# A transformer block with local dilated attention and a SiLU MLP: other tiles for the modulation weights, another order of loads and instructions

## The chip, the cores and the metric

The kernel runs on one core of a Trainium2 chip. The core has a matrix engine (TensorE, PE), a vector engine (VectorE, DVE), a scalar engine (ScalarE, ACT), a general one (GpSimd, POOL) and a sync engine (SyncE, SP) that here only issues DMAs. Each engine runs its own list of instructions in order and waits on semaphores. Data lie in SBUF (128 partitions); matmul results land in PSUM, which this kernel uses as eight banks of 128 x 512 floats. The metric is device time in microseconds of one execution.

## What is computed

The reference, cut to its core (S = 2048 tokens, D = 448, 16 heads of 28, F = 1792, all bfloat16):

```python
mod = (silu(c) @ w_mod).reshape(1, 6, 1, 448)      # w_mod: 448 x 2688
sa, ca, ga, sb, cb, gb = the six rows of mod
h = layernorm(x) * (1 + ca) + sa
# attention: each query sees 8 keys, at distances 0, 2, 4 ... 14 back
o = softmax(q . k[s - 2w] * 28**-0.5 over w = 0..7) . v
x = x + ga * (o @ wo)
h = layernorm(x) * (1 + cb) + sb
x = x + gb * (silu(h @ w1) @ w2)
```

Because the dilation is 2, even and odd tokens never meet: the kernel handles the two parities as two sequences of 1024.

## The kernel before

**Tiling.** The tokens are cut into four chunks of 512 (256 per parity). Attention runs in nine blocks of queries per parity; a block's keys are the 128 tokens up to its last query, so that a dense 128-key product and a 0/1 mask (`maskb`) replace the gather. A dimension of 448 is three tiles of 128 rows and a rest of 64. For the matmuls with D as the contracted side (QK, V, output projection, first MLP matmul) a helper `phases` runs pairs of 64-row matmuls, so that the rests of the two parities or the two halves of the output share a tile: this is why the rest of the QK weights is `wqk3`, two 64-row halves in one 128-row tile, and that of w1 is `w13`. The modulation weights `wmod`, in contrast, lie as four tiles of 112 rows (`KM = 112`).

**Stages.** First `c` goes through SiLU (`sc_op`), is turned into columns by a matmul (`c_cols`) and copied to `scT`; `mod_first` multiplies it with the first two of the six column groups of `wmod` (32 matmuls with one column each, L444), giving the shift and scale of the first layernorm (`modc`, L447/L448). Meanwhile the first chunk of tokens is normalised (statistics L497/L498 on VectorE or sums L501 and squares L507 on ScalarE, the power on GpSimd L513, the result `xn` L525/L527), transposed by PE (L564) and scaled into `h` (L571/L573). The later chunks are transposed by DMA (L588) and scaled by L593/L595. The QK weights are copied from `wqk` and `wqk3` into `wp` and `wp3`, in which each head of 28 columns is padded to 32 (`pad`, L603/L605; four copies, each on ScalarE or VectorE). QK is L668, its copies out of PSUM L672; V is L688 and L681. For each block and parity: logits L716, exponentials L724 on ScalarE, mask L748 and, after the product with V (L774), the division L779/L780 on VectorE, and a DMA transpose into `oT` (L784). The output projection L804 needs the `oT` of both parities and `wo`, which is multiplied by the gate `ga` (L916, with copies L917/L918); its result is added to x (L807). The MLP is L831, SiLU L839, L854 and the last addition L859 with the store L862; `w2` is multiplied by the gate `gb` (L920) two tiles at a time. The other four column groups of `wmod` are multiplied in `mod_late` (L463 into one row each, copied L477, spread to all partitions L468/L480 as gates, or turned to columns L475).

**Order.** Nothing schedules at run time. The kernel makes a list of 764 operations, and the string `ORDER` says in which order they are emitted, on which engine the ones with a choice run (suffix v for VectorE, a for ScalarE) and which PSUM banks they take (after slashes). The DMA issues of SyncE are in this order too; SyncE has eight completion semaphores for them, so the ninth DMA waits for an earlier one to land. The numbers in `load` and other operations (assumed durations) are read only by a planner that makes such a string; for a given `ORDER` they do nothing. On PE, a few matmuls on zeros (`junk`, L416) fill the wait at the beginning.

Before the change SyncE issues, in this order: first tokens of chunk 0, `wmod`'s first part in two loads (two of the four 112-row tiles each), the tokens of chunk 1, `wqk3`, V's weights in two loads, the QK weights in two, the tokens of chunks 2 and 3, the transposes of chunk 1, the second part of `wmod`, the transposes of chunk 2, `wo`, w2's first part, w1's first, and so on. ScalarE issues the other tokens of chunk 0 and then `c`.

The two loads with 64-row halves read DRAM with the two halves as the leading dimension:

```python
load(112, wqk3[:], dram(A_wqkv, 128, D, ((128, -D, 2), (1, 0, K3), (0, 1, D))), late)
load(224, w13[:], dram(B_w1, 128, F // 2, ((128, -F // 2, 2), (1, 0, K3), (0, 1, F // 2))), late, rate=0.3)
```

A second copy of the whole layer (`safe`) runs only where a softmax sum was out of range; it is not taken here.

Of the kernel before, what the change touches and what calls it, by code (L numbers as in the profile page):

```python
# [10 lines left out]
ALU = mybir.AluOpType  # L11
# [11 lines left out]
KM = D // KT  # L23
# [56 lines left out]
def half(j):  # L80
    return slice(K3 * j, K3 * j + K3)
# [156 lines left out]
def layer(ctx, tc, io, safe):  # L238
# [26 lines left out]

    NV, NP, NX, NO, NH = (4, 5, 2, 3, 3) if not safe else (4, 3, 2, 2, 3)
    x_all = ct([128, 4 * NC, D], "x_all")
    c4 = ct([KT, KM], "c4")
    sc4 = ct([KT, KM], "sc4")

    both = ct([128, 2 * NF * 512], "both")
# [752 lines left out]
```

## Time and profile before

| | us |
|---|---|
| median of three runs | 171.03 (170.42 to 171.82) |
| the profiled execution | 170.89 |
| its span, first to last instruction | 169.2 |
| PE busy | 160.8 |
| ScalarE busy | 116.4 |
| VectorE busy | 99.1 |

The profile is one execution. Its lines name the engine, the line of the code, what is written from what, the shape and the count; a time after an arrow is idle time of that engine and what ended it. A "chain of waits" is followed back from the last instruction, at each step to what released it. A matmul's duration in a row is modelled from start to end, and neighbours overlap, so the rate of a group is read from a row of the chain or from the distance of its start to that of the next group. The tables of stages give for each engine its busy microseconds and its number of instructions, then the granted clock of PE, the share in which the 16 DMA engines were busy, and GB/s.

### The profile page before, as it was taken

What the parts mean: (1) busy time and instruction counts of PE and PEld (TensorE: products, weight loads), DVE (VectorE), ACT (ScalarE), POOL (GpSimd) and SP (SyncE); (2) the same over time, 40 slices, a digit from 0 to 9 for tenths busy, and PEclk for the clock granted to TensorE, in tenths of its full rate; (3) what the DMA queues carried; (4) which work ended last, traced back from release to release, by engine and by line L of the source; (5) the groups of instructions that cost most, each with busy time, mean ns of one, the idle gap of its engine ahead of it and who ended that gap; (6) DMA issues with size and microseconds to landing.
All of it is one profiled execution on the core that took longest, in us unless ns stands there. A gap on an engine that the chain in (4) does not pass through costs nothing.

```text
span 169.2 us, 4278 instructions
## 1 busy us (share of the span) xinstructions
PE 160.8 (95%) x1763; PEld 79.9 (47%) x1764; DVE 99.1 (59%) x259; ACT 116.4 (69%) x166; POOL 15.5 (9%) x38
## 2 busy tenths in 40 slices
PE   7878999999999999999999999999999999999990
PEld 2344444353465554554464454564444454444670
DVE  2788899999988859475476309972950405100120
ACT  3676999899779967879996989484429903248000
POOL 4313112010000410011000000021001100000000
PEclk9999999999999999999999999999999999999999
DMA  5994999859994453500614001226410061100022
GB/s 180 251 324 171 190 303 164 265 154 101 142 248 109 112 103 76 169 0 9 119 27 111 2 0 31 54 63 117 113 54 6 0 124 38 49 0 0 27 62 68
DMA packets 32312, 17.48 MB, mean 103 GB/s; under 512 B 24157, under 2 KB 31453, under 8 KB 32285
## 3 DMA queue, kind: packets, MB, share of 16 engines
q1 hardware_dynamic: 32132, 16.90, 42.9%
q8 instruction: 16, 0.26, 0.7%
q10 hardware_dynamic: 152, 0.23, 0.4%
q14 instruction: 12, 0.09, 0.2%
HBM read 9.12 MB, written 1.84 MB: 65 GB/s over the span
## 4 chain that ended last, share of the span: by engine, by line
PE 74%; DMA 9%; DVE 7%; ACT 5%; issue 2%; SPq 0%
PE psum L831 25%; PE psum L854 24%; PE psum L804 7%; PE psum L668 6%; DMA wqk<-in_A_wqkv_dram 5%; PE psum L688 4%; PE psum L774 4%; PE psum L716 2%; DMA x_all<-in_A_x_dram 2%; DMA oT<-o 2%; DVE p L748 2%; PE psum L885 2%; ACT both L501 1%; ACT wp L603 1%; DVE wqk L595 1%
## 5 line engine op out<-in xcount | busy, mean ns | idle before, releaser
L831 PE MATMUL psum<-h,w 64*128 64x512 bf16 x392 | 43.7, 376 | 0.0
L854 PE MATMUL psum<-w,both 128*128 128x448 bf16 x210 | 42.1, 353 | 0.0
L839 ACT ACTIVATE both<-psum 128x1024 bf16<-128x1024 f32 x28 | 27.3, 1021 | 13.6 <-PE psum L831 13.6
L724 ACT ACTIVATE p<-psum 128x896 bf16<-128x896 f32 (+1 forms) x36 | 31.7, 935 | 5.0 <-PE psum L716 4.7
L831 PEld LDWEIGHTS <-w 64*128 64x128 bf16 x392 | 19.3, 94 | 22.2 <-issue 0.7
L854 PEld LDWEIGHTS <-both 128*128 128x128 bf16 x210 | 19.6, 98 | 19.1 <-issue 1.6
L513 POOL TENSOR_TENSOR rs<-rs,negh 128x2 f32<-128x2 f32 x16 | 12.5, 778 | 118.0 <-DVE rs L510 82.6
L748 DVE TENSOR_TENSOR p<-p,maskb 128x1792 bf16<-128x1792 bf16 (+1 forms) x18 | 19.5, 1099 | 4.8 <-ACT p L724 4.8
L859 DVE TENSOR_TENSOR ot<-psum,x_all 128x448 bf16<-128x448 f32 x15 | 9.2, 618 | 20.2 <-PE psum L854 15.9
L668 PE MATMUL psum<-h,wp 64*128 64x512 bf16 x168 | 19.8, 377 | 0.5 <-ACT wp L603 0.4
L668 PEld LDWEIGHTS <-wp 64*128 64x128 bf16 x224 | 10.4, 94 | 12.8 <-ACT wp L603 0.9
L507 ACT ACTIVATE mrow<-x_all,mv 128x448 bf16<-128x448 bf16 x16 | 10.7, 668 | 3.4 <-DVE mv L504 3.0
L804 PE MATMUL psum<-wo,oT 64*128 64x448 bf16 x112 | 12.7, 350 | 0.1
L593 ACT ACTIVATE h<-h,modc 128x512 bf16<-128x512 bf16 x7 | 5.5, 806 | 10.2 <-DMA h<-xn 10.2
L672 ACT CAST qk<-psum 128x1024 bf16<-128x1024 f32 x12 | 12.0, 1018 | 0.6 <-PE psum L668 0.6
L688 PE MATMUL psum<-wv,h 64*128 64x448 bf16 x98 | 11.3, 350 | 1.2 <-DMA wv<-in_A_wqkv_dram 1.1
L807 DVE SCALAR_TENSOR_TENSOR x_all<-psum,x_all 128x448 bf16<-128x448 f32 x16 | 9.5, 619 | 3.6 <-PE psum L804 3.6
L780 DVE TENSOR_TENSOR o<-psum,rc 112x448 bf16<-112x448 f32 (+1 forms) x18 | 11.2, 624 | 0.6
L779 DVE RECIPROCAL rc<-psum 112x16 f32<-112x16 f32 (+1 forms) x18 | 4.5, 251 | 10.2 <-PE psum L774 9.5
L774 PEld LDWEIGHTS <-p 128*128 128x128 bf16 x288 | 8.2, 96 | 3.3 <-issue 1.7
L774 PE MATMUL psum<-v,p 128*128 128x29 bf16 x288 | 9.0, 176 | 0.0
L595 DVE TENSOR_SCALAR h<-h,modc 128x512 bf16<-128x512 bf16 x17 | 6.1, 406 | 4.8 <-DMA h<-xn 4.6
(95 smaller groups left out, 144.6 us busy)
## 6 DMA issues: line engine op xcount, KB each, us to landing
out_dram<-ot SPq DMA_DIRECT2D x16, 112.0 KB, 1.8
both<-in_w_mod_dram SPq DMA_DIRECT2D x1, 1568.0 KB, 8.4
x_all<-in_A_x_dram SPq DMA_DIRECT2D x3, 448.0 KB, 8.1
w<-in_B_w_dram SPq DMA_DIRECT2D x3, 448.0 KB
w<-in_B_w_dram SPq DMA_DIRECT2D x1, 896.0 KB, 7.0
both<-in_w_mod_dram SPq DMA_DIRECT2D x2, 392.0 KB, 5.7
w<-in_B_w_dram SPq DMA_DIRECT2D x1, 672.0 KB, 5.4
wv<-in_A_wqkv_dram SPq DMA_DIRECT2D x2, 224.0 KB, 8.5
```

The source lines that it names most:

```text
L513: G.tensor_tensor(out=rs[:, j:j + n], in0=rs[:, j:j + n], in1=negh[:, 0:n], op=ALU.pow)
L668: return T.matmul(ps[:, j, :], lhsT=w.rearrange("p h d -> p (h d)"), rhs=h[rows, :, t, 128:128 + CP], start=start, stop=stop)
L672: copy_on(o)(out=qk[:, :, g, :, s0:s0 + CP], in_=ps.rearrange("p j (t s) -> p j t s", t=2))
L688: T.matmul(ps[:, par, 0:D], lhsT=h[rows, par, t, b0:b0 + 128], rhs=wv[rows, t, :], start=start, stop=stop)
L724: S.activation(out=out_, in_=ps[:, :, 0:4 * nq].rearrange("p j (g q) -> p j g q", q=nq), func=ACTF.Exp, scale=SCALE)
L748: V.tensor_tensor(out=p, in0=p, in1=maskb[:, 1 if b == 0 else 0, 0:nq].unsqueeze(1).to_broadcast([128, H, nq]), op=ALU.mult)
L774: T.matmul(ps[:, h, 0:DH + 1], lhsT=p[:, at:at + 128], rhs=v[:, h, 0:DH + 1], start=True, stop=True)
L780: V.tensor_tensor(out=box["o"][0:nq, off:off + D].rearrange("p (h d) -> p h d", d=DH), in0=ps[0:nq, :, 0:DH], in1=r.unsqueeze(2).to_broadc ...
L804: T.matmul(ps[par][:, 0:D], lhsT=oT[rows, t, par, s0:s0 + 128], rhs=wo[rows, par, t, :], start=start, stop=stop)
L831: return T.matmul(ps[:, j, :], lhsT=w, rhs=h[rows, :, t, :], start=start, stop=stop)
L839: silus[k].append(P.op(("act", 904.0), lambda o, i=i, box=box: S.activation(out=hid[:, k % 2, :, i, :], in_=box["ps"], func=ACTF.Silu), [m ...
L854: T.matmul(box["ps"][:, 0:D], lhsT=hid[:, k % 2, f % 2, f // 2, 128 * j:128 * j + 128], rhs=w2[:, f // 2 + 7 * (f % 2), :], start=(f == 0) ...
```

## The change

`wmod`'s 448 rows become three tiles of 128 and one of 64 (`KM = 64` is now the width of a piece of `c`, of which there are seven, turned into columns by two matmuls). The fourth tile's other 64 rows are set to zero by two new memsets of VectorE, and the modulation matmuls contract over 128 rows. The first and the second part of `wmod` are each two loads, one of three tiles and one of 64 rows. `wqk3` and `w13` are loaded by two DMAs each, one for each half. The tokens of chunk 1 are issued after V's weights, those of chunks 2 and 3 in one load; two 448 KB loads of w1 become one, and the two of w2 become one. ScalarE issues `c` ahead of the tokens, and its SiLU table is loaded before its first sum, so that one table load less stands at the beginning. `ORDER` is another string: all engines' lists change.

```diff
-KM = D // KT
+KM = 64
...
-    c4 = ct([KT, KM], "c4")
-    sc4 = ct([KT, KM], "sc4")
+    c4 = ct([D // KM, KM], "c4")
+    sc4 = ct([D // KM, KM], "sc4")
...
+    V.memset(wmod[half(1), 3, 0:2 * D], 0.0)
     V.memset(wp[:, :, :, DH:32], 0.0)
...
+    V.memset(wmod[half(1), 3, 2 * D:6 * D], 0.0)
...
-    act_q = [P.op(("none", 0.0), lambda o: nc.scalar.dma_start(**first_x(1)))]
-    act_q.append(P.op(("none", 0.0), lambda o: nc.scalar.dma_start(out=c4[:], in_=c.rearrange("o (k p) -> (o k) p", p=KM)), act_q[-1:]))
+    act_q = [P.op(("none", 0.0), lambda o: nc.scalar.dma_start(out=c4[:], in_=c.rearrange("o (k p) -> (o k) p", p=KM)))]
+    act_q.append(P.op(("none", 0.0), lambda o: nc.scalar.dma_start(**first_x(1)), act_q[-1:]))
...
-    def load_mod(k0, k1, c0, c1, after=()):
-        return load((c1 - c0) * (k1 - k0) * KM / 512, wmod[0:KM, k0:k1, c0:c1], w_mod[KM * k0:KM * k1, c0:c1].rearrange("(k p) n -> p k n", p=KM), after)
+    def load_mod(c0, c1, after=()):
+        kb = (c1 - c0) * 0.75
+        return [load(kb, wmod[:, 0:3, c0:c1], rows3(w_mod[:, c0:c1]), after), load(kb / 6, wmod[half(0), 3, c0:c1], w_mod[384:D, c0:c1], after)]
...
-    ld_ma = [load_mod(0, 2, 0, 2 * D, late), load_mod(2, 4, 0, 2 * D, late)]
+    ld_ma = load_mod(0, 2 * D, late)
...
-    ld_qk = [[a], [b], [a], [load(112, wqk3[:], dram(A_wqkv, 128, D, ((128, -D, 2), (1, 0, K3), (0, 1, D))), late)]]
+    ld_qk = [[a], [b], [a], [load(56, wqk3[half(a), :], A_wqkv[128 * (a + 1):128 * (a + 1) + K3, D * (1 - a):D * (2 - a)], late) for a in range(2)]]
...
-    ld_x += [[load(448, x_all[:, 4 * k:4 * k + 4, :].rearrange("p (i t) d -> p i (t d)", t=2), x_view[k], late)] * 2 for k in range(1, NC)]
-    ld_m2 = [load_mod(0, 4, 2 * D, 6 * D, late)]
+    ld_x.append([load(448, x_all[:, 4:8, :].rearrange("p (i t) d -> p i (t d)", t=2), x_view[1], [x["deps"][0] for x in ld_v])] * 2)
+    ld_x += [[load(896, x_all[:, 8:16, :].rearrange("p (k i t) d -> p k i (t d)", i=2, t=2), x_view[2:4].rearrange("c p i n -> p c i n"), late)] * 2] * 2
+    ld_m2 = load_mod(2 * D, 6 * D, late)
...
-    ld_1 = [load(448, w1[:, k, :], B_w1[r:r + 128, :], late, rate=0.3) for k, r in ((0, 0), (2, 320))]
+    ld_1 = [load(896, w1[:, 0:3:2, :], dram(B_w1, 0, 0, ((1, 0, 128), (320, 0, 2), (0, 1, F))), late, rate=0.3)]
...
-    ld_1.append(load(224, w13[:], dram(B_w1, 128, F // 2, ((128, -F // 2, 2), (1, 0, K3), (0, 1, F // 2))), late, rate=0.3))
-    ld_2 = [load(112.0 * (f1 - f0), w2[:, f0:f1, :], B_w2[128 * f0:128 * f1, :].rearrange("(f p) d -> p f d", p=128), late, rate=0.3) for f0, f1 in ((0, 8), (8, NF))]
+    ld_1 += [load(112, w13[half(a), :], B_w1[128 * (a + 1):128 * (a + 1) + K3, F // 2 * (1 - a):F // 2 * (2 - a)], late, rate=0.3) for a in range(2)]
+    ld_2 = [load(112.0 * (f1 - f0), w2[:, f0:f1, :], B_w2[128 * f0:128 * f1, :].rearrange("(f p) d -> p f d", p=128), late, rate=0.3) for f0, f1 in ((0, NF),)]
...
-        T.matmul(box["c"][0:KM, 0:KT], lhsT=sc4[:], rhs=ident[0:KT, 0:KT], start=True, stop=True)
+        for i in range(2):
+            T.matmul(box["c"][half(i), 0:KT], lhsT=sc4[:], rhs=ident[0:D // KM, i:2 * KT:2], start=True, stop=True)
...
-    m_a = P.op(("pe", 420.0), lambda o: mod_first(o, 0, 2), [sct, ld_ma[0]], take=("one",))
-    m_b = P.op(("pe", 420.0), lambda o: mod_first(o, 2, 4), [m_a, ld_ma[1]])
+    m_a = P.op(("pe", 630.0), lambda o: mod_first(o, 0, 3), [sct, ld_ma[0]], take=("one",))
+    m_b = P.op(("pe", 220.0), lambda o: mod_first(o, 3, 4), [m_a, ld_ma[1]])
```

What the new `ORDER` does, as far as the prediction speaks of it. SyncE: first tokens, `wmod` (three tiles), `wmod` (64 rows), V's weights (two loads), tokens of chunk 1, the smaller QK load, `wqk3` in two, the larger QK load, the tokens of chunks 2 and 3, the transposes of chunk 1; later, of block 0's two transposes into `oT`, the one of the odd parity first. ScalarE: three of the four padding copies in a row (two before), then both V copies, four sums, squares, and one more V copy ahead of the first exponential; one of the two copies of the gates. VectorE: one padding copy instead of two; between the first mask and the division of block 0's second parity it has also block 1's mask and division for the first parity, and one V copy, one copy of the gates and one halo copy (L656) less. PE: all four QK groups of the third chunk (three before) and one more block of logits stand ahead of the first output projection.

More of the change, by code (lines that the diff above doesn't have):

```diff
@@ L361, in load @@
     def load(kb, out, in_, after=(), rate=0.36):
[L362 removed]
+        return sp(450.0 if kb < 300 else 620.0, lambda o: nc.sync.dma_start(out=out, in_=in_), [begin] + list(after), 500.0, dma=(600.0, 1300.0, 150.0 + kb / rate))[0]
     def first_x(i):
         return dict(out=x_all[:, 2 * i:2 * i + 2, :].rearrange("p t d -> p (t d)"), in_=x_view[0, :, i, :])
[L368 to L374 removed]
+    act_q = [P.op(("none", 0.0), lambda o: nc.scalar.dma_start(out=c4[:], in_=c.rearrange("o (k p) -> (o k) p", p=KM)))]
+    act_q.append(P.op(("none", 0.0), lambda o: nc.scalar.dma_start(**first_x(1)), act_q[-1:]))
+    ld_c = [P.op(("none", 3900.0), lambda o: S.preload_act_table(ACTF.Silu), act_q[-1:])]
+    ld_x = [[load(224, **first_x(0)), P.op(("none", 4800.0), none, act_q[-1:])]]
+    def load_mod(c0, c1, after=()):
+        kb = (c1 - c0) * 0.75
+        return [load(kb, wmod[:, 0:3, c0:c1], rows3(w_mod[:, c0:c1]), after), load(kb / 6, wmod[half(0), 3, c0:c1], w_mod[384:D, c0:c1], after)]
     late = [P.op(("sp", 1100.0), none, [ld_x[0][0]["deps"][0]])]
[L377 removed]
+    ld_ma = load_mod(0, 2 * D, late)
     late = [x["deps"][0] for x in ld_ma]
@@ L428, in c_cols @@
         box["c"] = onet()
-        T.matmul(box["c"][0:KM, 0:KT], lhsT=sc4[:], rhs=ident[0:KT, 0:KT], start=True, stop=True)
+        for i in range(2):
+            T.matmul(box["c"][half(i), 0:KT], lhsT=sc4[:], rhs=ident[0:D // KM, i:2 * KT:2], start=True, stop=True)
     cc = P.op(("pe", 60.0), c_cols, [sc_op], take=("one",))
-    sct = P.op(("act", 60.0), lambda o: S.copy(out=scT[0:KM, :], in_=box["c"][0:KM, 0:KT]), [cc], give=((cc, "one"),))
-    rep = P.op(("dve", 130.0), lambda o: V.tensor_copy(out=screp[0:KM], in_=scT[0:KM, :].unsqueeze(2).to_broadcast([KM, KT, 32])), [sct])
+    sct = P.op(("act", 60.0), lambda o: S.copy(out=scT[:], in_=box["c"][:, 0:KT]), [cc], give=((cc, "one"),))
+    rep = P.op(("dve", 130.0), lambda o: V.tensor_copy(out=screp[:], in_=scT[:].unsqueeze(2).to_broadcast([128, KT, 32])), [sct])
     box1 = {}
@@ L443, in mod_first @@
                     c0 = a * D + ROW[j]
-                    T.matmul(box1["ps"][:, a, j:j + 1], lhsT=wmod[0:KM, k, c0:c0 + 128], rhs=scT[0:KM, k:k + 1], start=(k + a + j == 0), stop=(k + a + j == 2 * KT - 1))
+                    T.matmul(box1["ps"][:, a, j:j + 1], lhsT=wmod[:, k, c0:c0 + 128], rhs=scT[:, k:k + 1], start=(k + a + j == 0), stop=(k + a + j == 2 * KT - 1))
     def mod_out(dst0, shift, scale):
@@ L462, in rows @@
                 for j, v in enumerate((2, 5, 3, 4)):
-                    T.matmul(box["r"][32 * j:32 * j + 32, 0:D], lhsT=screp[0:KM, k, :], rhs=wmod[0:KM, k, v * D:(v + 1) * D], start=(k == 0), stop=(k == KT - 1))
+                    T.matmul(box["r"][32 * j:32 * j + 32, 0:D], lhsT=screp[:, k, :], rhs=wmod[:, k, v * D:(v + 1) * D], start=(k == 0), stop=(k == KT - 1))
         def gates(o):
```

7 lines of the change are left out of this document (2 added, 5 removed), and 46 rows, old and new, of the table ORDER.

## The prediction

> **What bounds the kernel now.** I read the page first: its head, its busy shares, its forty slices.
>
> ```profile
> span 169.2 us, 4278 instructions
> ...
> PE 160.8 (95%) x1763; PEld 79.9 (47%) x1764; DVE 99.1 (59%) x259; ACT 116.4 (69%) x166; POOL 15.5 (9%) x38
> ...
> PE   7878999999999999999999999999999999999990
> ...
> DVE  2788899999988859475476309972950405100120
> ACT  3676999899779967879996989484429903248000
> ...
> PEclk9999999999999999999999999999999999999999
> ```
>
> TensorE (PE) is busy 95% of the span and "9" in every slice from the fourth on, at full granted clock. VectorE (DVE) and ScalarE (ACT) are at 9 only in slices 4 to 10, so roughly from 12 to 45 us. Next I asked for busy time in stages, to see where PE still loses anything.
>
> ```profile
> 0.00:7.80 7.80, 5.89 (x17) 2.03 (x17) 3.97 (x20) 4.22 (x8) 2.73 (x14) 1.00 0.78 210
> 7.80:12.16 4.36, 2.99 (x52) 2.07 (x52) 3.69 (x15) 2.70 (x6) 1.44 (x8) 1.00 1.08 313
> 12.16:16.00 3.84, 3.29 (x30) 1.57 (x31) 2.98 (x13) 2.52 (x5) 1.38 (x2) 1.00 0.66 235
> ...
> 40.00:44.00 4.00, 3.88 (x53) 1.49 (x54) 3.97 (x10) 3.39 (x5) 0.00 (x0) 1.00 0.82 167
> 44.00:60.00 16.00, 16.00 (x254) 8.65 (x252) 12.89 (x35) 14.24 (x22) 2.19 (x2) 1.00 0.71 135
> ```
>
> From 44 us on PE has no idle time: what is left there is a fixed amount of matmul work, and only its start can move. Before that it is idle 0.55 us in 12.16 to 16 and 0.12 in 40 to 44. So the question is by how much the change brings forward the point from which PE never waits again. The chain of waits, printed in order of time, says what sets that point.
>
> ```profile
> 4.87 9.14 DMA wqk<-in_A_wqkv_dram
> ...
> 14.03 1.78 ACT wp L603 x2
> ...
> 36.63 0.27 DVE rc L779
> ...
> 36.92 0.62 DVE o L780
> ...
> 38.37 0.97 DVE p L748
> 39.34 3.02 DMA oT<-o
> ...
> 42.41 0.93 PE psum L804 x7
> 43.33 0.31 PE psum L716 x16
> ...
> 59.33 3.02 PE psum L668 x28
> ```
>
> Read upwards from the first output projection (L804) at 42.41: it waits for the transposed attention output (oT); that for VectorE's divisions (L779/L780, the second ending at 38.37); those, through a chain of VectorE and ScalarE work, for ScalarE's copies of the QK weights (L603) at 14.03; and those for the load of the QK weights, issued at 4.87, landed 9.14 us later. From 42.41 on the chain is PE alone.
>
> **The head.** Three consumers show what the loads cost.
>
> ```profile
> 12.16 3.27 PE L688 MATMUL psum<-wv,h 64*128 64x448 bf16 x28 [1.05 <-DMA wv<-in_A_wqkv_dram]
> ...
> 15.86 7.97 PE L668 MATMUL psum<-h,wp 64*128 64x512 bf16 x70 [0.43 <-ACT wp L603]
> ...
> 28.29 1.22 DVE L748 TENSOR_TENSOR p<-p,maskb 128x2048 bf16<-128x2048 bf16 x1
> ```
>
> PE begins V at 12.16, after 1.05 us of waiting for V's weights, and QK at 15.86, after 0.43 of waiting for the padded QK weights. V's weights now go ahead of 448 KB of tokens, so V no longer waits for them. It starts when h is ready.
>
> ```profile
> 1.26 4.88 PE L416 MATMUL psum<-both 128*128 128x512 bf16 x11 [1.26 <-DVE both L313]
> ...
> 5.14 1.28 ACT L370 ACT_TABLE_LOAD   x1
> ...
> 6.92 1.04 PE L416 MATMUL psum<-both 128*128 128x512 bf16 x4
> ...
> 9.46 2.84 ACT L571 ACTIVATE h<-psum,modc 128x256 bf16<-128x256 bf16 x6 [2.03 <-PE psum L564]
> ```
>
> h comes from ScalarE at 9.46, when the modulation columns and the transposes are there. A table load of 1.28 us at 5.14 falls out, since c comes first and one table serves both uses; the variance sums then come earlier. The modulation load for it has the same bytes with 448 KB of tokens no longer directly behind it. I take 0.5 us for h (from 0, if the modulation load lands as before, to 1.28, the whole table load). V then runs from about 11.0 (four of the six h pieces, 4 x 0.47, after 9.0) for at most the 3.27 us of now, to 14.3. This is worth nothing by itself, because QK waits for its weights anyway; the cover is that load, and were it gone V's end would set QK's start, 1.6 us earlier than now.
>
> QK's weights are the last of x 448, modulation 784, tokens 448, V 448 and QK 784 KB in both orders: 2912 KB, 2.98 MB. The first two stages moved 7.80 x 210 + 4.36 x 313 = 3.00 MB by 12.16. So by bytes alone QK's weights could have been there by about 12.2; the copy started at 14.03 nevertheless, and DMA was running at full rate at that time, for transfers issued later:
>
> ```profile
> 13.00:14.00 1.00, 1.00 (x14) 0.62 (x12) 0.91 (x5) 0.00 (x0) 0.71 (x2) 1.00 1.06 378
> 14.00:15.00 1.00, 1.00 (x14) 0.61 (x11) 0.27 (x1) 0.97 (x2) 0.65 (x1) 1.00 0.39 142
> ```
>
> So parts of the awaited load lagged behind later ones. The old 64-row rest of the QK weights is one load of two 64-row halves; the new one is two loads of 64 rows. Bounds for the new landing: 12.2 (no lag) and 14.0 (lag as before); I take 13.0, about the middle: the rows show that the lag belongs to some loads and not to the byte count, but not that the new rest is free of it. The Trainium skill ("DMA: Bandwidth & Descriptors", on why a DMA increments its semaphore by 16) says that a DMA runs on the largest number of engines up to 16 that divides the slowest dimension of both sides: the old rest, with a DRAM side led by a dimension of 2, would use two engines, the new ones 16. By that rule the lag goes and the landing is 12.2, and the total 0.8 us below mine; the stage rows agree that something lagged, but no row here shows which engines.
>
> Then ScalarE pads three tiles in a row, all behind that landing, where it had two: 1.78 us for two (chain, 14.03), and for the third, half as wide, about half of one, 0.5 (VectorE's pair has 0.25 against 0.39):
>
> ```profile
> 13.56 0.25 DVE L605 COPY wp<-wqk 128x448 bf16<-128x448 bf16 x1
> ...
> 14.73 0.39 DVE L603 COPY wp<-wqk 128x896 bf16<-128x896 bf16 x1 [0.79 <-DMA wqk<-in_A_wqkv_dram]
> ```
>
> QK starts at 13.0 + 1.78 + 0.5 + 0.06 = 15.3, or 0.5 earlier than 15.86 (14.5 to 16.3 by the bounds).
>
> At no cost: VectorE's two new memsets are two and four times the words of this one, 0.48 + 0.96 = 1.44 us,
>
> ```profile
> 1.53 0.24 DVE L320 MEMSET wo<- 64x224 uint32 x1
> ```
>
> and lie in the 1.9 us in which VectorE waits for the first tokens (uncovered, 1.4 us ahead of the first statistics):
>
> ```profile
> DVE st L497 <- DMA x_all<-in_A_x_dram: 1.9, 1, 1.9
> ```
>
> The second matmul on c and the zero rows of the fourth modulation tile lie in PE's idle head, as does the second tokens' later landing: its statistics now stand behind the two h pieces on VectorE (0.69 us), which fills that wait. Two more DMA issues stand ahead of SyncE's first transposes, which wait for VectorE. The w1 and w2 loads, merged, are due only by the MLP after 65 us; if they were late, the MLP would wait for them.
>
> **To the first projection.** ScalarE's stretch from the first pad to the first exponential took 26.01 - 14.03 = 11.98 us, practically without a gap. In the new order it also holds the third pad (0.5) and one more V eviction, 0.85 of its 0.90 (they overlap a little):
>
> ```profile
> 15.71 0.90 ACT L681 CAST v<-psum 128x896 bf16<-128x896 f32 x1
> ...
> 26.01 1.94 ACT L724 ACTIVATE p<-psum 128x1024 bf16<-128x1024 f32 x2
> ```
>
> First exponential at 13.0 + 11.98 + 1.35 = 26.3, end at 28.3. That is when VectorE's first mask began before (28.29), so from there I compare VectorE's two lists. Before: 28.29 to 38.37, 10.1 us, up to the second division. New: one mask more (0.97), one division more (0.27 + 0.62 = 0.9), the two small copies of modulation columns (0.15 together, an estimate, below the 0.27 of one reciprocal); less one V eviction, one copy of the gates and one halo copy:
>
> ```profile
> 32.93 1.15 DVE gbc L480 x2
> ...
> 35.40 0.20 DVE wqk L656
> ...
> 35.67 0.91 DVE v L681
> ```
>
> that is 0.97 + 0.9 + 0.15 - 0.91 - 0.58 - 0.20 = +0.3. The second division of block 0 ends at 28.3 + 10.1 + 0.3 = 38.7; I add 0.2, because PE puts eight QK matmuls (8 x 0.108 = 0.86) ahead of that block's values: 38.9. SyncE now has the later parity's transpose first, so the other one queues behind it:
>
> ```profile
> 37.57 2.95 SPq L784 DMA_TRANSPOSE oT<-o  x2
> ```
>
> The pair ended at 37.57 + 2.95 = 40.52 and the second began at 39.34 (chain), so one issue takes 1.2 us. The second would begin at 38.9 + 0.1 + 1.2 = 40.2 and land 3.02 later, as it did from 39.34: oT is complete at 43.2, the projection runs at 43.3, 0.9 us later than before. But PE has done more by then: 14 QK matmuls, 14/28 of 3.02 = 1.51, and one more block of logits, 0.31. **Sum:** 43.3 - (42.41 + 1.82) = -0.9 us. Behind it the same work remains, with no idle time in before. The new order has its own waits there, which no row shows: from 0 to 0.6 (as much as it lost in 12.16 to 16); I take 0.1. That leaves -0.8. The profiled execution took 170.89 (span 169.2 and 1.7 around it), 0.14 below the median of 171.03. So 170.1 for the execution and, the difference being less than the spread of the three runs, 170.2 for the median.
>
> **Rivals.** First, the early landing: QK's weights at 12.2 move pads, exponentials and divisions by 0.8, oT lands at 42.5, and -0.9 becomes -1.7; with the waits of 0.6 that PE lost in 12.16 to 16 gone too, -2.3. With the 0.1 that is 168.8 to 169.4. For it: the byte count, and PE could be there: from QK's start to 42.41 it took 26.55, so 14.5 + 26.55 + 1.82 less those waits is 42.3. Against: nothing shows that these loads can run without a lag. Second, ScalarE's extra load decides, and the kernel becomes slower. Up to the end of block 1's exponentials the new ScalarE list has, beyond the pad and the V eviction (1.35), one copy of the gates (0.58 on VectorE) and a sum of squares in place of a QK eviction, which I set against each other: 1.9 in all. The new order puts block 1's mask and division (0.97 + 0.9) ahead of block 0's second division, which before depended on nothing of block 1. If the weights land at 14.0, all of 1.9 + 0.97 + 0.9 comes on top of 38.37: 42.1, projection 4.4 later as in my sum (43.3 after 38.9), 46.5, and 46.5 - 44.2 = +2.3: 173.3. It decides once the second division of block 0 ends after 39.9, where the sum is zero. For it: both engines at 9 in slices 4 to 10. Against: VectorE has other work to fill with. Third, the landing stays at 14.0 and the rest goes as in my sum: division at 39.9, no change, 171.0; that is the case in which the change does not do what it is made of.
>
> Fourth, the clock. PE now stands still from V's end, 14.3, to 15.3, 1 us or somewhat more. Before, it had 0.8 us with one tiny matmul in it between the first eleven warm-up matmuls, which end at 6.14, and the next four at 6.92; these took 0.26 us each, the first eleven 0.44: that gap did not slow the clock. The Trainium skill ("TensorE: Matmul & The Clock Gate", Part 1) puts the idle window that halves the clock at about 3.4 us, and the free-running window could catch a shorter gap only in part. If the clock were halved, a burst of QK would take up to twice as long until it recovers: with the 4.88 us that the warm-up took, 2.4 us lost, -0.8 + 2.4 = +1.6, 172.6.
>
> **Numbers.** What a measurement of this kernel can tell from no change is about 1%, 1.7 us. Chances: forecast 0.42 (169.5 to 170.8 with the waits behind the projection and half of the landing's bounds), early landing 0.23 (168.8 to 169.4), ScalarE 0.22 (171.2 to 173.3), landing unchanged 0.10 (171.0), clock 0.03 (172.6). Faster by over 1%, below 169.3, is most of the early case and the edge of the forecast: 0.21 + 0.04 = 0.25. Slower by over 1%, above 172.7, is the upper part of ScalarE, where both engines are as full as they were, and half of the clock: 0.15 + 0.02 = 0.17. Within: 0.58. The range leaves out the edge of the early case and the upper end of ScalarE, together less than 0.2: 168.7 to 172.8.
>
> **What would show it.** Right: pads begin on ScalarE at 12.2 to 13.5 and QK at about 15.3; V starts by 11.2 and PE idles about 1 us before QK; the first exponential at 26.3; the first projection at 43.3, with all four QK groups of the third chunk behind it, where it had three, and no PE idle after. Wrong: pads at 14.0 (no lag removed), a projection after 44.3 (ScalarE or VectorE decides), matmuls of 0.43 us after the gap (clock), or PE idle beyond 45 us, which the sum holds at 0.1.

## The result and the profile after

The changed kernel took 172.57 us (median of 22 runs, 171.54 to 173.74), the kernel before 171.53 on the same chips (22 runs, 170.07 to 174.12). The ratio is 1.0079, with a 95% interval of 1.0052 to 1.0107: slower by 0.8%, where I had forecast 0.5% faster. The ratio compares fast executions alone, so it isn't the quotient of the two medians. The profiled execution took 172.96 us. The head of its page, with busy time and the forty slices:

```profile
span 171.2 us, 4283 instructions
...
PE 162.0 (95%) x1764; PEld 79.6 (46%) x1765; DVE 101.7 (59%) x260; ACT 116.0 (68%) x166; POOL 18.0 (11%) x38
...
PE   7799999899997999999999999999999999999990
...
PEclk9969999999999999999999999999999999999999
```

The span is 171.2 us against 169.2. PE has the same work (162.0 us busy against 160.8, of which a part is the slow clock of the third slice), so the 2 us more are idle time, lost clock, and a little that the profile counts as busy. The table of stages, with the same borders as before, shows where (span of the stage, busy time of PE, PEld, DVE, ACT and POOL with their counts, clock, DMA share, GB/s):

```profile
7.80:12.16 4.36, 4.14 (x35) 2.52 (x35) 3.92 (x17) 2.13 (x7) 1.00 (x2) 0.61 1.07 361
12.16:16.00 3.84, 3.54 (x34) 1.25 (x32) 3.62 (x15) 3.84 (x8) 2.24 (x9) 1.00 0.33 116
...
28.00:40.00 12.00, 11.52 (x202) 5.45 (x196) 10.97 (x23) 10.65 (x16) 2.92 (x1) 1.00 0.66 194
...
44.00:60.00 16.00, 14.53 (x244) 7.48 (x234) 12.96 (x31) 13.09 (x20) 0.69 (x1) 1.00 0.64 161
```

The last row is the one to see. From 44 to 60 us PE was busy for 16.00 us before and is now busy for 14.53. That is the last sign of being wrong that the prediction named: PE idle beyond 45 us. The chain of waits in order of time (start, us, what) names three transfers behind the head, where it had one:

```profile
1.42 4.90 DMA x_all<-in_A_x_dram
...
25.79 4.54 DMA wqk<-xn
31.16 1.01 DVE v L686
...
45.12 4.03 DMA h<-xn
51.79 3.81 DMA oT<-o
55.73 0.91 PE psum L809 x7
```

The end now hangs on chunk 2's transposes (issued at 25.79) and behind them VectorE's V eviction, on chunk 3's transposes (45.12), and on the middle blocks' `oT` (51.79) for the second output projection at 55.73. The waits from 16 to 62 us say the same from the side of each engine (who, for whom; us, times, longest):

```profile
ACT h L598 <- DMA h<-xn: 1.6, 1, 1.6
...
DVE h L600 <- DMA h<-xn: 0.8, 1, 0.8
DVE wqk L600 <- DMA wqk<-xn: 0.8, 1, 0.8
PE psum L673 <- ACT v L686: 0.6, 1, 0.6
...
PE psum L809 <- DMA oT<-o: 0.6, 1, 0.6
...
PE psum L673 <- DVE v L686: 0.4, 1, 0.4
```

VectorE and ScalarE stand still for transposes, and the evictions queued behind (L686) make PE wait in its turn.

### The profile page after: what moved, and what is told of

Same layout as the page of the kernel before. It is cut to its first block, busy times and chain, and to the rows that moved or that the text cites. A ratio compares the mean times of both kernels' runs of the same rounds, so it can differ in the third digit from the quotient of the medians.

```text
span 171.2 us, 4283 instructions
## 1 busy us (share of the span) xinstructions
PE 162.0 (95%) x1764; PEld 79.6 (46%) x1765; DVE 101.7 (59%) x260; ACT 116.0 (68%) x166; POOL 18.0 (11%) x38
## 4 chain that ended last, share of the span: by engine, by line
PE 80%; DMA 10%; ACT 3%; DVE 3%; issue 1%; ACTq 0%; DVEq 0%
PE psum L836 25%; PE psum L859 24%; PE psum L673 11%; PE psum L809 6%; PE psum L779 4%; PE psum L693 3%; DMA x_all<-in_A_x_dram 3%; PE psum L721 3%; DMA wqk<-xn 3%; DMA h<-xn 2%; DMA oT<-o 2%; PE psum L890 2%; ACT wp L608 1%; PE psum L569 1%; ACT h L576 1%
## 5 line engine op out<-in xcount | busy, mean ns | idle before, releaser
L836 PEld LDWEIGHTS <-w 64*128 64x128 bf16 x392 | 18.8, 94 | 22.7 <-issue 0.4
L518 POOL TENSOR_TENSOR rs<-rs,negh 128x2 f32<-128x2 f32 x16 | 14.9, 932 | 116.5 <-DVE rs L515 79.1
L673 PE MATMUL psum<-h,wp 64*128 64x512 bf16 x168 | 20.6, 377 | 1.5 <-ACT v L686 0.6
L673 PEld LDWEIGHTS <-wp 64*128 64x128 bf16 x224 | 10.0, 94 | 14.4 <-issue 2.3
L512 ACT ACTIVATE mrow<-x_all,mv 128x448 bf16<-128x448 bf16 x16 | 10.6, 666 | 5.2 <-DVE mv L509 5.0
L598 ACT ACTIVATE h<-h,modc 128x512 bf16<-128x512 bf16 x8 | 6.2, 806 | 8.9 <-DMA h<-xn 8.9
L677 DVE CAST qk<-psum 128x1024 bf16<-128x1024 f32 x7 | 8.5, 1218 | 1.2 <-PE psum L673 1.1
```

The costliest lines, as they stand in the source:

```text
L512: S.activation(out=scratch, in_=x_all[:, us[j], :], func=ACTF.Square, bias=mv[:, j, 0:1], scale=ROOT, accum_out=mv[:, j, 1:2])
L518: G.tensor_tensor(out=rs[:, j:j + n], in0=rs[:, j:j + n], in1=negh[:, 0:n], op=ALU.pow)
L673: return T.matmul(ps[:, j, :], lhsT=w.rearrange("p h d -> p (h d)"), rhs=h[rows, :, t, 128:128 + CP], start=start, stop=stop)
L836: return T.matmul(ps[:, j, :], lhsT=w, rhs=h[rows, :, t, :], start=start, stop=stop)
```

## The experiments

Every kernel was timed in five rounds beside the kernel before. The table gives what the runs below refer to: the ratio with its interval, and from the one profile of each kernel the start of the first QK matmul, the time from it to the first projection's first matmul and to the end. A profile is a single execution and can lie over 1 us from its kernel's median (run 3's took 172.59 us against a median of 171.36, run 8's 173.32 against 172.10), so a ratio and a profile need not agree. The split at the first QK matmul separates the loads and the head from the order behind. The time to the projection compares only kernels of one order, since the new one does 1.82 us more of PE's work ahead of it.

| kernel | ratio to before | first QK | to projection | to the end |
|---|---|---|---|---|
| before | 1 | 15.86 | 26.08 | 153.31 |
| changed | 1.0079 (1.0052 to 1.0107) | 15.36 | 28.93 | 155.80 |
| 1 new loads, old order | 1.0045 (1.0014 to 1.0076) | 16.03 | 25.91 | 153.62 |
| 2 old loads, new order | 1.0239 (1.0200 to 1.0279) | 17.29 | 30.22 | 157.29 |
| 3 changed, wo later | 0.9998 (0.9972 to 1.0023) | 14.77 | 28.86 | 156.01 |
| 4 changed, h transposes together | 1.0056 (1.0021 to 1.0092) | 14.21 | 29.01 | 155.67 |
| 5 head new, rest old | 1.0078 (1.0038 to 1.0118) | 14.41 | 28.12 | 156.16 |
| 6 as 1, tokens first | 0.9900 (0.9853 to 0.9947) | 13.84 | 26.05 | 154.73 |
| 7 as 4, division first | 1.0035 (1.0005 to 1.0066) | 14.16 | 29.26 | 155.99 |
| 8 changed again | 1.0038 (1.0005 to 1.0070) | 14.89 | 29.30 | 156.72 |
| 9 changed, V eviction first | 1.0001 (0.9968 to 1.0035) | 14.05 | 28.38 | 155.55 |
| 10 changed, five moves | 0.9982 (0.9949 to 1.0014) | 15.28 | 28.38 | 154.88 |
| 11 as 6, w1 later | 0.9826 (0.9782 to 0.9870) | 13.82 | 25.91 | 153.17 |
| 12 before, rests split | 0.9909 (0.9878 to 0.9940) | 14.95 | 25.77 | 153.30 |
| 13 changed, tokens first | 1.0066 (1.0029 to 1.0103) | 14.13 | 29.16 | 156.45 |
| 14 as 10, tokens first | 0.9981 (0.9950 to 1.0012) | 14.07 | 28.38 | 154.69 |
| 15 as 11, Silu first | 0.9858 (0.9812 to 0.9903) | 13.29 | 25.99 | 152.98 |

In the diffs an order's entries are operations by number; a load's two numbers are its issue and its landing.

**1 and 2: loads and order taken apart.** Each load's number in the one order is replaced by those of the loads that take its place.

```diff
 run 1: tiles and loads of the changed kernel, ORDER of before
-22 16 18 20 12 14 24 26 28
+24 16 18 20 22 12 14 26 28 30
 run 2: tiles and loads of before, ORDER of the changed kernel
-20 22 24 14 18 16 12 26 30 28
+18 20 22 14 16 12 24 26 28
```

> All of the change's tiles, zero fills and loads, with the order of before (each load in the place of the one that it replaces; the first tokens still behind c on ScalarE). Theory 1, the new order makes the 2 us of new stalls behind 15.3 us and the loads give 0.5 us: span about 168.7 (0.5 below before's 169.2), ratio to before 0.994 to 1.000, QK's weights land at about 13.0, no stall of QK in front of chunk 3. Theory 2, the loads themselves (merged, and so longer, in front of the DMA transposes) hold up the transposes: ratio 1.005 or more, chunk 2's transposes land over 4 us after issue and the second projection waits. Theory 3, c first on ScalarE costs through the late first tokens and the clock: V still starts late, near 11.9, and the ratio is over 1.

> Before's tiles and loads (QK's rest in one load, wmod in 112-row tiles, tokens of chunks 1 to 3 in single loads, w1 and w2 in two) in the new order. Theory 1 (the order): ratio to before 1.008 to 1.016, with the same PE stalls at chunk 3's first QK (near 50.5) and at the second projection (near 54.8) as in the changed kernel; QK's weights land at about 14.0 and QK starts near 15.9 or later. Theory 2 (the merged loads): ratio within 0.997 to 1.004, and these two stalls shrink to under 0.3 us together.

Run 1 has hardly any of the loss behind QK (153.62 us), so the order makes it. The ratio of 1.0045 is nevertheless above theory 1's 1.000, and theory 3 fits: the head is late, V at 12.87 and the first QK matmul at 16.03. The waits of its first 17 us show why: the load of PE's weights for the matmul on c waits 2.7 us for Silu, which in this order stands behind ScalarE's first sum over the tokens (L506), and these now come behind c. The granted clock was also halved from 8.7 to 12.1 us in this profile, which may have its part in the late head.

```profile
PEld L434 <- ACT sc L428: 2.7, 1, 2.7
```

Run 2 is slower than either kernel, and above the 1.016 that theory 1 allowed. It has the changed kernel's stalls (157.29 us behind QK) and a head of its own making, with QK at 17.29. In its waits the padding copies of whole QK tiles (L603) wait 2.5 us for the weights (1.3 in before), while the rest's own copy (L605) waits for nothing:

```profile
ACT wp L603 <- DMA wqk<-in_A_wqkv_dram: 2.5, 1, 2.5
```

In the changed kernel, with the rests in two loads, no copy waits. So the new order needs the new loads at this place, and the cost of the order is not run 2's ratio.

**3 and 4: two single suspects, `wo`'s load and chunk 3's transposes.**

```diff
 run 3: wo's 336 KB load (32) behind chunk 2's transposes (201, 203)
-57 113a 32 197 198
+57 113a 197 198
...
-200v 203 204 171v
+200v 203 32 204 171v
 run 4: chunk 3's second h transpose (248) ahead of the third oT transpose (304)
-346 309 304 295 248 249 250
+346 309 248 304 295 249 250
```

> The changed kernel, the 336 KB load of wo put back behind chunk 2's two transposes on SyncE (one place in the order). If the early wo load is what makes the second transpose land 4.54 us after its issue instead of the 3.5 of before: landing at about 29.3 instead of 30.33, VectorE's wait from 29.64 to 30.42 gone, third division of block 0's two parities done by about 39.1 instead of 39.83, first projection near 43.5 to 43.9 instead of 44.29; what of it reaches the end depends on the stalls behind, so the ratio to before would be 1.003 to 1.008. If the landing is late for another reason (wmod's second half, still ahead of it, or the transposes being issued back to back): landing still at 30.0 or later and ratio 1.008 as it was.

> The changed kernel with one place in SyncE's order changed: chunk 3's second h transpose ahead of block 0's third oT transpose instead of behind it (as before had it). Theory 1: it issues at about 43.8 instead of 45.12, lands near 47.8 instead of 49.17; VectorE's wait from 48.44 to 49.24 and ScalarE's from 47.64 to 49.23 go, PE's stall of about 1.1 us in front of chunk 3's first QK goes, and so most of the wait for the second projection's oT; span 0.8 to 1.3 us shorter than the changed kernel's 171.2, ratio to before 1.000 to 1.004. Rival: the third oT transpose, now 1.3 us later, or the w1 load behind it becomes the next wait, and the second projection waits as long as it did: ratio 1.006 to 1.010.

Run 3's profile shows no earlier projection (28.86 us behind QK), so in that execution the load in front of the transposes is not what delays them. Its ratio is lower than the changed kernel's all the same, and the intervals of runs 3 and 8 overlap (to 1.0023, from 1.0005). The profiled execution was the slowest of run 3's twelve and needn't show what made the others faster. That stays open. Run 4 went as its rival said: PE's wait in front of chunk 3's QK (`L673 <- ACT v L686`) fell from 0.61 to 0.30 us, and the second projection's wait for `oT` grew from 0.55 to 0.84.

**5 and 6: the head apart from the rest, and tokens first.**

```diff
 run 5: changed kernel's ORDER up to chunk 0's last QK matmul (107), then before's
 run 6: run 1, and
-    act_q = [... c4 ...]; act_q.append(... first_x(1) ...)
+    act_q = [... first_x(1) ...]; act_q.append(... c4 ...)
```

> The changed kernel's tiles and loads, its order up to the last of chunk 0's QK matmuls, and from there before's order for all that is left. The first four runs had the time from the first QK matmul to the end at 153.3 (before), 153.6 (new loads, old order) and 155.7 to 156.0 us (the three with the new order and loads), and the first QK matmul of these three at 14.2 to 15.4. Theory 1 (the order behind chunk 0's QK costs 2.4 us, the head with its loads gains about 1): 153.3 to 154.0 us from the first QK matmul to the end, first QK matmul at 14.2 to 15.4, ratio to before 0.992 to 0.999. Rival (the head's order itself, with wo's load early, is what later stalls come from): 154.8 us or more behind QK, ratio 1.002 or more.

> Before's order with the new tiles and loads, and ScalarE's two loads as before had them (first tokens, then c). In the first run with old order V started at 12.87, late, since ScalarE's first square waited for the tokens behind c and Silu stood behind it. Theory 1: without that, V starts at 11.0 to 12.2, the QK weights' split alone brings the first QK matmul to 15.0 to 15.6 (before 15.86), 153.3 to 153.8 us behind it, ratio 0.995 to 1.000. Rival (what brings QK forward is the new order of the loads, not the split): first QK matmul at 15.8 or later, ratio 1.000 to 1.004.

Run 5 doesn't decide: where the two orders were joined, PE waits 2.0 us for a QK eviction, so its 156.16 us is no measure of the head.

```profile
PE psum L673 <- DVE qk L677: 2.0, 1, 2.0
```

Run 6 is the first kernel that beats both: V starts at 10.41 instead of 12.16, QK 2.0 us earlier. It is even under the ratio of 0.995 that theory 1 allowed, although it gives 1.4 us back behind QK (154.73 us, expected 153.8 at most), in one wait at its second projection. The stages, and PE's waits between 13 and 62 us:

```profile
44.00:60.00 16.00, 14.54 (x214) 7.73 (x212) 11.13 (x29) 12.83 (x20) 2.61 (x2) 1.00 0.79 159
```

```profile
PE psum L809 <- ACT qk L677: 1.5, 1, 1.5
```

**7 and 8: one more move, and the changed kernel once more.** Run 7 is run 4 with a division (328) ahead of chunk 3's first scale and shift pass (253); run 8 has no edit.

```diff
-320 378 253v 327/3 328
+320 378 327/3 328 253v
```

> The changed kernel with chunk 3's two h transposes together on SyncE (as in the fourth run) and, on VectorE, one division of the middle blocks ahead of the first of chunk 3's scale and shift passes instead of behind it. In the fourth run the stall in front of chunk 3's QK fell by 0.4 and the second projection's wait for oT rose by 0.3. Theory 1: now the third and fourth oT transposes issue 0.5 to 0.9 earlier, the second projection's wait falls from 1.0 to under 0.4; from the first QK matmul to the end 154.8 to 155.3 instead of 155.7, ratio to before 1.000 to 1.004. Rival (the wait moves on once more, to chunk 3's scale and shift passes or the next transposes): 155.5 or more, ratio 1.005 or more.

> The changed kernel as it is, for a second profile and for times on the chip of the others: 155.6 to 156.1 us from the first QK matmul to the end by each theory that puts the loss into the order, first QK matmul anywhere from 14.2 to 15.4, ratio to before 1.005 to 1.011. If the ratio is nearer to 1.000 here, then the third run (wo's load later, ratio 0.9998) owed its gain to the chip and not to its edit.

Run 7 changed nothing behind QK (155.99 us). Its `oT` transposes went out at 47.74, 49.03 and 50.34, and PE still waited 0.73 us for the last. Run 8 confirms the loss behind QK (156.72 us, above the 156.1 expected) and shows how the head varies: QK began at 14.89 here, at 15.36 in the first profile, with the same instructions. Its ratio of 1.0038 is below the expected 1.005, about halfway to run 3's: so part of run 3's gain may be the chip's and not its edit's.

**9 and 10: the three waits.**

```diff
 run 9: block 2's V eviction (180) ahead of chunk 2's scale and shift passes (207, 209)
-285/1/2 34 207v 286 287 179 209v 180v
+285/1/2 34 286 287 179 180v 207v 209v
 run 10: run 9, the moves of 4 and 7, and
-252a 254v 380 321
+252a 254v 321
...
-224 225a 379
+224 225a 380 379
...
-296 297 38 319/2
+296 297 319/2
...
-311 313 312
+311 313 38 312
```

> The changed kernel with one place of VectorE's order changed: the eviction of block 2's V stands ahead of chunk 2's first two scale and shift passes instead of behind them. In the two profiles of the changed kernel VectorE waits 0.8 us there for chunk 2's transposes, and TensorE waits 0.55 and 0.93 us near 31 us for that eviction. Theory 1 (the order makes the stalls): the stall near 31 us is under 0.2 us, from the first QK matmul to the first projection 28.2 to 28.6 us instead of 28.9 to 29.3, to the end 155.0 to 155.6 instead of 155.8 and 156.7, ratio to before 1.000 to 1.003. Rival (what is gained is lost again at the next waits, for chunk 3's transposes and the second projection's oT, which hang on DMA and not on VectorE): first projection earlier, second projection's wait longer by as much, end as before, ratio 1.004 or more.

> The changed kernel with five moves in its order: the V eviction of the run beside this, chunk 3's h transposes together, one division ahead of chunk 3's scale and shift passes, ScalarE's square of block 0's second normalisation behind the two evictions of chunk 2's last V blocks, and the 448 KB load of w1 behind the middle blocks' three oT transposes instead of ahead of them. Theory 1: all three places of TensorE's new stalls (near 31, 50 and 54 us) shrink to under 1.0 us together from 2.6 (profile of the changed kernel) and 3.1 (its second one), from the first QK matmul to the end 153.6 to 154.6 us, ratio to before 0.991 to 0.998. Rival (the order's loss lies in the amount of work between the landmarks, or in DMA, not at these three waits): 155.2 us or more, ratio 1.000 or more.

Run 9 did what theory 1 said up to the first projection (28.38 us instead of 28.93 and 29.30) and kept it: ratio 1.0001. The row of the V eviction is gone from PE's waits between 13 and 62 us, the two later ones are there as they were:

```profile
PE psum L809 <- DMA oT<-o: 0.7, 1, 0.7
PE psum L673 <- ACT v L686: 0.6, 1, 0.6
```

Run 10 also took away the wait in front of chunk 3's QK. The ratio (0.9982) and the 154.88 us behind QK fall just short of theory 1. What is left is mostly `oT`, and it is longer:

```profile
PE psum L809 <- DMA oT<-o: 0.9, 1, 0.9
```

Of 156.3 us behind QK (mean of the changed kernel's two profiles) run 10 has 154.9, and before has 153.3: the moves took back about half. That half of the order's loss was at these waits; of the 1.6 us left, the last wait is 0.9.

**11 and 12: the loads in the old order.**

```diff
 run 11: run 6, with w1's merged 896 KB load (36) behind the 448 KB one (38)
-247 336/2/1 36 37 295
+247 336/2/1 295
...
-268/3 38 378
+268/3 38 36 37 378
 run 12: before, and
-[load(112, wqk3[:], ...)]
+[load(56, wqk3[half(a), :], ...) for a in range(2)]
 and the same for w13
```

> The sixth kernel (old order, new loads, tokens first; ratio 0.990) with the merged 896 KB load of w1 put behind the 448 KB one on SyncE, so that four oT transposes no longer stand behind it. The sixth kernel waits 1.46 us at its second projection; its fourth oT transpose issued at 49.12 and the projection went on at 53.74. If the merged load in front delays the transposes: landing about 1 us earlier, the wait under 0.6 us, 153.5 to 154.0 us from the first QK matmul to the end instead of 154.73, ratio 0.981 to 0.988. If the wait is there because all work ahead of it came 2 us earlier while the transposes take the time that they take: wait still over 1.1 us, ratio 0.988 to 0.992.

> The kernel before with nothing changed but the two 64-row rests (wqk3 and w13), each loaded in two loads. Theory of the prediction (the rest, on two engines, is what the first QK matmul waits for): the first QK matmul at 14.0 to 15.3 instead of 15.86, V's start as in before (near 12.2), ratio to before 0.991 to 0.998. Rival (the 128-row tiles of wmod bring all of the head forward, V's start with it, and the rest is hidden): first QK matmul at 15.6 or later, ratio 0.998 to 1.003.

Run 11 took run 6's wait away altogether. PE has no idle time from 44 to 60 us, and from QK to the end it takes 153.17 us:

```profile
44.00:60.00 16.00, 16.00 (x230) 8.36 (x226) 12.76 (x32) 14.22 (x22) 2.62 (x2) 1.00 0.74 152
```

So the merged load, with four `oT` transposes issued behind it, was that wait. The transposes show it themselves. From issue to landing, the shortest, median and longest of the four were, in run 6, then in run 11:

```profile
DMA to landing us min/median/max: 5.2/6.1/6.9
```

```profile
DMA to landing us min/median/max: 2.3/3.0/4.3
```

The row of run 6 names ScalarE, whose eviction ended just then; in run 11 the projection begins at 52.32, before that eviction (52.91), so it doesn't hang on it. With several semaphores awaited, the one named need not be the one that cost. Run 12 shows what the split rest is worth alone, 0.9%. The start of its padding copies and of QK, by the timeline:

```profile
12.88 1.77 ACT L603 COPY wp<-wqk 128x896 bf16<-128x896 bf16 x2
...
13.82 0.39 DVE L603 COPY wp<-wqk 128x896 bf16<-128x896 bf16 x1
...
14.95 0.81 PE L668 MATMUL psum<-h,wp 64*128 64x512 bf16 x6
```

No row of it has an idle time in brackets: neither ScalarE nor VectorE waits for the weights any more, where in before VectorE waited 0.79 us and ScalarE 1.3.

**13, 14 and 15: c in front, alone.** Runs 13 and 14 swap ScalarE's two loads as run 6 does, in the changed kernel and in run 10. Run 15 is run 11 with Silu (69) and its table load (3) ahead of the first sum (88), which the expectations of runs 13 and 15 call a square.

```diff
-63 66 88 3 69 89
+63 66 3 69 88 89
```

> The changed kernel with ScalarE's two loads swapped back (tokens, then c), its order kept, so Silu still stands ahead of the first square. In eight profiles with c in front the first square starts at 5.63 to 6.83 and the first QK matmul at 14.05 to 15.36, 8.42 to 8.60 later but for one. If c in front costs the head its spread and its lateness: first square at 4.5 to 5.2, V at 9.6 to 10.6, first QK matmul at 13.2 to 14.0, ratio to before 0.996 to 1.001 instead of 1.004 to 1.008. Rival (c, now behind the tokens, becomes late itself and holds Silu, the modulation and with it V): square at 5.5 or later, first QK matmul at 14.3 or later, ratio 1.003 or more.

> The tenth kernel (new order with five moves, ratio 0.998) with the same swap. If head and order add up: 154.5 to 155.2 us from the first QK matmul to the end as there (154.88), first QK matmul at 13.2 to 14.0, ratio 0.989 to 0.994; still over the 0.983 of the old order with the new loads, since about 1 us of wait for oT at the second projection is left. If what comes earlier in the head is lost at that wait, which hangs on transposes: wait over 1.5 us, ratio 0.996 or more.

> The eleventh kernel (old order, new loads, tokens first, w1's merged load behind; ratio 0.983) with Silu ahead of the first square on ScalarE, as in the new order, so that one table load of 1.28 us falls away. If the modulation is what V waits for: V at 9.7 to 10.2 instead of 10.39, ratio 0.978 to 0.983. If wmod's landing or the tokens bound V: V at 10.3 or later, ratio 0.982 to 0.986.

In run 13 V began at 9.77, as expected, but QK only at 14.13, and the ratio (1.0066) did not fall. In its waits from 8 to 15 us ScalarE waits for the weights, and PE for the padding copies, of which ScalarE has three in a row:

```profile
PE psum L673 <- ACT wp L608: 1.1, 1, 1.1
...
ACT wp L608 <- DMA wqk<-in_A_wqkv_dram: 0.4, 1, 0.4
```

Run 14 confirms it (0.9981 against 0.9982 without the swap; its projection waits no longer than run 10's). Run 15's head is earlier still (QK at 13.29), but its ratio can't be told from run 11's. Runs 13 and 15 have the same tiles and loads, tokens and Silu in the same sequence, and differ in the order and w1's place in it: 1.0066 and 0.9858, and 3.5 us behind QK.

## Why the prediction was wrong

**The landing of QK's weights** was mis-sized in the cautious direction. I took 13.0 between 12.2 and 14.0. By the landings that the traces record, the last of QK's weights was there at 11.65 in the changed kernel (run 8: 12.27; before: 14.64). In run 13 ScalarE gets to the padding copies early enough to wait for the weights, 0.4 us, and begins at 11.83. The first rival's 12.2 was nearer, and the Trainium skill's rule that it stood beside ("DMA: Bandwidth & Descriptors", on the 16 increments) was borne out: run 12 changes only how the two rests are loaded, by the rule from two engines to 16, and 15.86 becomes 14.95. The engines themselves aren't named in a row, but the landings fit two of them: before's one load of the rest leaves three records, one soon after its issue (3.90) and two at its end (11.43 and 11.55), where the head's other loads of 128 rows leave 16 each, and so does each of run 12's two rest loads. The rest was not late for its own copy (L605 waited in neither kernel); it held up the loads behind it. V's two loads landed 8.5 us after their issue in before (median) and 6.3 in run 12, and QK's whole tiles followed. In the changed kernel's own profile QK began at 15.36, as forecast (15.3), but by an accident: its first pad at 13.05 waited for no load, it stood behind ScalarE's h copies.

**h was late, where I had it earlier.** The prediction put the later landing of chunk 1's tokens into PE's idle head, and that held. For ScalarE's tokens of chunk 0, which now stand behind c, it had no price at all: it let the variance sums come earlier, and h with them. The chain has these tokens on the path (1.42, 4.90 us): the first sum over them began at 6.34 instead of 4.46, ScalarE's first h piece at 9.75 instead of 9.46, and V at 11.89 instead of the 11.0 forecast. Part of it is the halved clock: run 8, with the same instructions, full clock and the sum even later (6.52), has V at 11.21, and QK 8.4 us behind the sum instead of 9.0. So the clock cost about 0.6 to 0.9 us here (an estimate from these two profiles). The eight profiles with this head have that sum between 5.63 and 6.83 and QK between 14.05 and 15.36. In the old order c in front cost 1.5% (runs 1 and 6; part of it may be run 1's clock); in the new one, by run 13, nothing that can be measured, since the three pads stand behind.

**Up to the first projection** the sum had 28.0 us from QK (43.3 - 15.3); the trace has 28.93, the second one 29.30. The first exponential (26.45, forecast 26.3) and the first mask (28.42, forecast 28.3) came as the sum had them. The step that failed compares VectorE's lists entry by entry, "10.1 + 0.3" (10.6 with the 0.2 for the QK matmuls). Between the mask and the end of block 0's second division the trace has 39.83 - 28.42 = 11.4 us. The sum had no term for the wait of 0.8 us for chunk 2's transposes, which in the new order stand in front of a V eviction that PE needs:

```profile
28.42 1.22 DVE L753 TENSOR_TENSOR p<-p,maskb 128x2048 bf16<-128x2048 bf16 x1
30.42 0.73 DVE L600 TENSOR_SCALAR wqk<-wqk,modc 128x512 bf16<-128x512 bf16 x2 [0.78 <-DMA wqk<-xn]
...
39.21 0.62 DVE L785 TENSOR_TENSOR o<-psum,rc 128x448 bf16<-128x448 f32 x1
```

The break-even that I gave, a division that ends after 39.9, was met almost exactly (39.83), and the gain up to there was about zero (44.29 against 42.41 + 1.82 = 44.23). Run 9 takes the one eviction out from behind that wait and has 28.38.

**Behind the projection** is the step that decides the sign: "from 0 to 0.6; I take 0.1". PE's idle time from 44 to 60 us is 16.00 - 14.53 = 1.47 in the first profile and 1.72 in the second. That is most of what the changed kernel loses from there on: 126.87 us from the projection to the end, against 124.94 in before (from 42.41, as the prediction counts, and without the 1.82 of work that moved ahead). The order puts chunk 3's transposes apart, with evictions behind the passes that wait for them, and three blocks' divisions and transposes one behind the other in front of the second projection. From the first QK matmul on the forecast had -0.3 (-0.8 less the 0.5 of QK's start); the trace has 155.80 - 153.31 = +2.5, and -0.5 for QK's start: +2.0, the difference of the spans. Of the 2.5, 1.85 is PE's idle time (6.45 us from the first QK matmul to the end, 4.60 in before); the rest the profile counts as busy, and the ends of matmuls are modelled.

**The rivals.** The second, slower by ScalarE's and VectorE's load, had the right sign and a wrong mechanism: these engines were not too full, they stood and waited (the first three rows of the waits of 16 to 62 us). What spoke for it, "both engines at 9 in slices 4 to 10", was also misread: in before VectorE is at 9 in slices 6 to 11 and 16, and ScalarE in 5 to 7, 9, 10 and again in later ones, up to slice 32. The clock did fall in the head of this profile (0.61 from 7.8 to 12.16), not after V but behind the modulation's small matmuls, in front of which PE had waited 0.98 us; it made the head late, as said above. The second profile has no such dip and loses more behind QK, so it isn't the cause of the loss there.

**What stays open.** Behind QK runs 10 and 14 are still 1.6 and 1.4 us above before. Their wait for `oT` is 0.9 and 0.8 of it; that it comes from there being too little PE work between the three blocks' values and the second projection is argued from the order and was not tried. Of the other 0.6 to 0.7 us, 0.2 lies behind the last matmul (4.23 and 4.25 us from ScalarE's last copy to the end, 4.03 in before); the rest was not traced, nor was run 3's lower ratio.

## What to carry to other kernels

A change that mends loads and re-plans everything at once should be taken apart at a landmark that both versions have: here the loads in the old order, two of them placed otherwise than in the changed kernel (ScalarE's tokens ahead of c, w1 later), are worth 1.7% (run 11), and the order took more than that back. When an order is new, look in it for each transfer that an engine waits for and read what stands behind that wait on the same engine; a list of durations doesn't show it. And a merged load isn't only an issue less: transposes issued behind it landed later (6.1 us after issue instead of 3.0), 1.5 us of PE's time in run 6 and none in run 11.

## What was not expected of the hardware

The clock was halved early in four profiles, for about 3.4 us each time: from 8.1 us on in the changed kernel, 8.9 in run 12, 8.7 in run 1 and 17.3 in run 2. In run 12 it came behind a wait of 0.91 us of PE in front of the matmul on c (stages of 1 us; the clock is the number ahead of the DMA share), and PE was busy for 78 to 100% of each stage. A wait of this length doesn't explain it: run 5 waited 1.19 us in front of the same modulation matmuls as the changed kernel, which had 0.98, and kept its full clock. The Trainium skill ("TensorE: Matmul & The Clock Gate", Part 1) puts the idle window at about 3.4 us; no PE wait here was that long. What brought the clock down stays open.

```profile
8.00:9.00 1.00, 0.94 (x34) 0.86 (x31) 0.54 (x3) 0.00 (x0) 1.00 (x7) 0.97 1.11 285
9.00:10.00 1.00, 0.78 (x9) 0.72 (x7) 0.93 (x5) 0.40 (x1) 0.26 (x2) 0.50 1.12 307
...
12.00:13.00 1.00, 1.00 (x9) 0.42 (x10) 0.97 (x5) 0.97 (x4) 0.07 (x1) 0.82 1.07 374
```

And the landing of the first tokens varies by more than 1 us: the sum that waits for them began anywhere from 5.63 to 6.83 us in eight profiles of seven kernels with the same head, and the first QK matmul mostly moved with it (8.42 to 8.60 us later but for one).
